# Experts of a pair moved from the last stage of the next pair to the first stage two pairs on, with another split of the first stage's blocks

## The chip, the cores and the metric

One NeuronCore of one Trainium2 chip runs the whole program. The metric is device time in microseconds (us) of one execution; of several runs the median is given. The engines are TensorE (PE, with its weight loads as PEld), VectorE (DVE), ScalarE (ACT), GpSimd (POOL) and the queue engine SyncE (SP), which issues most transfers.

## The reference

A causal convolution along the sequence by FFT, and then a mixture step that changes 128 rows of each sequence.

```python
B, S, D = (8, 6336, 128)          # F = 1024, capacity = 128
Yf = np.fft.rfft(x, n=2 * S, axis=1) * np.fft.rfft(h, n=2 * S, axis=0)[None]
x = np.fft.irfft(Yf, n=2 * S, axis=1)[:, :S, :]
scores = np.einsum('bsd,d->bs', x, w_gate)
out = x.copy()
for b in range(B):
    top_idx = np.argpartition(-scores[b], capacity)[:capacity]
    xe = x[b, top_idx]
    ye = np.maximum(xe @ w1, 0.0) @ w2
    g = 1.0 / (1.0 + np.exp(-scores[b, top_idx]))
    out[b, top_idx] = x[b, top_idx] + g[:, None] * ye
```

## The kernel before

The sequence index is split as n = 64 * n1 + n2, with 99 values of n1 and 64 of n2. Two sequences are worked on at a time, so there are four pairs (`g` = 0 to 3). All products are f32. Each pair goes through four stages, and the order in which instructions stand on every engine is the order in which the Python code writes them: nothing is rescheduled, and each engine takes its instructions strictly in that order. Generators that `yield` are interleaved by `mix(main, (other, rate), ...)`: after each step of `main`, each other generator advances by `rate` steps on the average.

- `stage_a` (products over n1, L159). Its unit is a block of 8 columns of one sequence. POOL turns a block into the buffer `xt` (L143, three buffers, turned up to two blocks ahead), PE multiplies it by `fa` in two steps of 8 matmuls, and ACT or DVE evicts each step's PSUM bank into `slots` (L61 or L63). `acts` is the pattern of who evicts: 1 is ACT, 0 is DVE. A block is named by its half (which sequence of the pair) and by u (which half of the columns). There are 32 blocks in a pair, so 64 steps.
- `stage_b` (products over n2, L57 with the table `w`), 25 steps for each u. Each step needs a table and a piece of the filter's spectrum from HBM, through SP; ACT and DVE multiply by the spectrum (L209, L210, L214), and DVE or POOL adds (L221).
- `stage_c` (products with `wc`, L57), 32 steps for each u, evicted by L61.
- `stage_d` (products over k1 with tables `at`, L247), 32 steps. Each is evicted by ACT (L251), written to `out`, multiplied by `w_gate` on POOL (L255) and summed on DVE (L257). These sums are the scores `ss` of the mixture step.

The mixture step of pair g is the generator `side`, and it runs beside the stages of pair g+1. `pick` finds the 128 largest scores by two searches of eight steps. A step is a chain of DVE compare and reduce (L286, L289), a small PE product with `ones` (L57, into a bank `m` of its own), and three DVE instructions (L293 to L300). `pick` has 28 yields in all. `gather` then fetches the chosen rows with an indirect DMA (L393), and `feed` runs the expert for one sequence: a transpose (L404), 8 products with `w1` (L419), ReLU on ACT (L422), 8 products with `w2` (L427), and a scatter back with an indirect DMA from POOL (L430). Before the change `feed` follows `pick` at once, so the experts of pair g stand in stage d of pair g+1. The mixture step of the last pair has nothing to run beside, and it stands alone at the end of the program: the tail.

The order of a pair after the first is therefore: stage a alone (`part`, 21 blocks, with `side`); stage b for u = 0, with the other 11 blocks of stage a (`more`) between its steps; stage b for u = 1 with stage c for u = 0; stage c for u = 1; stage d.

The two sequences of a pair have their input tiles `xb[0]` and `xb[1]`, which are part of the tile `flat`, named `slots` in the profile. The array `zp` that stage d reads lies over `xb[1]`:

```python
xb = [flat[0:N1, i * XS:(i + 1) * XS].rearrange("p (n d) -> p n d", d=D) for i in range(2)]
yp = flat[:, 2 * XS:].rearrange("p (j k t) -> p j k t", k=N1, t=2)
zp = flat[0:N1, 2 * XS + N1 * 2 * D - ZS:].rearrange("p (j m t) -> p j m t", m=128, t=2)
```

With XS = 8192 and ZS = 32768, `xb[1]` takes the columns 8192 to 16383 and `zp` begins at column 8960. The second sequence of the next pair is loaded by `load_x(x[2 * g + 3], 1)`, which stands after stage d in the program. The first sequence is loaded a stage earlier.

## Time and profile before

| what | value |
|---|---|
| median of 3 runs | 1059.35 us (1058.58 to 1063.21) |
| the profiled execution | 1056.93 us, of which the span of its instructions is 1055.2 us |
| PE busy | 934.0 us (89%), PEld 850.0 us (81%) |
| DVE, ACT, POOL busy | 598.7 us (57%), 574.3 us (54%), 568.8 us (54%) |
| granted TensorE clock | 0.963 of full on the average |
| moved by DMA | 203.18 MB, 193 GB/s on the average |

Busy shares are averages over stages that have different limits. The stages of the pairs follow one another in time, so the trace can be cut at their borders, and each stretch can be read by itself: how long it is, how long each engine was busy in it, the granted clock (1.00 is 2.4 GHz, 0.50 is 1.2 GHz), and the share of the DMA engines' time that was used.

### The profile page before, as it was taken

Reading aid. Unit: us, or ns where it says so; the run is one execution under the profiler, and the core shown is the slowest. Engines: PE = TensorE matmul, PEld = TensorE weight load, DVE = VectorE, ACT = ScalarE, POOL = GpSimd, SP = SyncE. Lnnn points to the kernel's source line nnn. Section 1 sums busy time; section 2 is a strip of 40 time slices with the busy share of each in tenths; the row PEclk is TensorE's granted clock in tenths of the full one; section 3 lists DMA queues with packets and bytes.
Section 4 is the critical chain, followed back from the end, with each engine's and each line's share of the span. In section 5 each row is a group of like instructions: output and inputs, shape, how many; then the busy total and the mean of one; then the engine's idle time right before and its main releaser. Section 6 shows DMA issues by size and latency. Waiting matters only on the chain. (4 is left out here: it accounts for less than half of the span.)

```text
span 1055.2 us, 33274 instructions
## 1 busy us (share of the span) xinstructions
PE 934.0 (89%) x13740; PEld 850.0 (81%) x13740; DVE 598.7 (57%) x1183; ACT 574.3 (54%) x1038; POOL 568.8 (54%) x472
## 2 busy tenths in 40 slices
PE   2998889999999899989999999989999899989614
PEld 2998788997789889977789899967798899967504
DVE  0324677703366978533367978434468887343573
ACT  1324667773357877643367877633378786623201
POOL 2525676505767866126676955037686764056401
PEclk9998999999999999999999999999999999999856
DMA  8787999877775986325575976226567883046300
GB/s 275 256 263 196 248 249 243 227 236 237 251 235 161 298 274 206 144 69 174 158 257 166 309 259 201 102 85 201 171 205 245 275 287 103 2 134 191 99 0 11
DMA packets 121676, 203.18 MB, mean 193 GB/s; under 512 B 12903, under 2 KB 62282, under 8 KB 117962
## 3 DMA queue, kind: packets, MB, share of 16 engines
q1 hardware_dynamic: 94262, 174.05, 54.0%
q10 hardware_dynamic: 26752, 25.96, 7.5%
q8 instruction: 109, 1.79, 0.7%
q0 software_dynamic: 512, 1.05, 0.4%
q14 instruction: 41, 0.34, 0.1%
HBM read 168.05 MB, written 39.45 MB: 197 GB/s over the span
## 5 line engine op out<-in xcount | busy, mean ns | idle before, releaser
L61 ACT COPY slots<-p 128x396 f32<-128x396 f32 (+1 forms) x449 | 263.0, 587 | 130.5 <-PE p L159 63.4
L221 POOL TENSOR_TENSOR slots<-slots,tx 128x512 f32<-128x512 f32 x180 | 232.1, 1306 | 139.0 <-DVE tx L214 95.2
L255 POOL TENSOR_TENSOR tm<-hr,wg 99x512 f32<-99x512 f32 x128 | 161.6, 1275 | 205.3 <-ACT hr L251 169.7
L159 PE MATMUL p<-fa,xt 99*64 99x99 f32 x4608 | 226.8, 252 | 28.4 <-POOL xt L143 20.4
L57 PE MATMUL p<-wc,slots 128*64 128x128 f32 (+1 forms) x4096 | 246.3, 273 | 2.6 <-DVE slots L214 1.9
L57 PE MATMUL p<-slots,w 128*64 128x128 f32 x3168 | 223.2, 282 | 26.0 <-DMA w<-tab_wb 15.8
L159 PEld LDWEIGHTS p<-fa,xt 99*64 99x64 f32 x4608 | 214.5, 139 | 33.0 <-POOL xt L143 21.3
L247 PE MATMUL p<-slots,w 99*99 99x256 f32 x1024 | 231.7, 384 | 3.7 <-ACT slots L61 2.8
L57 PEld LDWEIGHTS p<-wc,slots 128*64 128x64 f32 (+1 forms) x4096 | 228.2, 126 | 5.0 <-DVE slots L214 2.7
L57 PEld LDWEIGHTS p<-slots,w 128*64 128x64 f32 x3168 | 190.0, 138 | 35.0 <-issue 16.2
L247 PEld LDWEIGHTS p<-slots,w 99*99 99x99 f32 x1024 | 168.1, 166 | 60.3 <-ACT slots L61 3.8
L143 POOL COPY xt<-slots 99x512 f32<-99x512 f32 x144 | 165.4, 1169 | 74.1 <-PE p L159 39.7
L257 DVE TENSOR_REDUCE sc<-tm 99x4 f32<-99x512 f32 x128 | 87.6, 686 | 202.7 <-POOL tm L255 202.7
L214 DVE TENSOR_TENSOR slots<-p,hr 128x512 f32<-128x512 f32 (+1 forms) x200 | 136.4, 682 | 80.3 <-ACT p L210 71.1
L251 ACT COPY hr<-p 99x512 f32<-99x512 f32 x128 | 75.0, 586 | 155.3 <-PE p L247 145.6
L209 ACT ACTIVATE p<-p 64x512 f32<-64x512 f32 (+1 forms) x200 | 113.1, 566 | 79.1 <-PE p L57 72.4
L214 DVE TENSOR_TENSOR tx<-p,hr 128x512 f32<-128x512 f32 (+1 forms) x200 | 135.0, 675 | 0.0
L210 ACT COPY p<-p 64x512 f32<-64x512 f32 (+1 forms) x200 | 110.8, 554 | 6.3
L63 DVE COPY slots<-p 128x396 f32<-128x396 f32 (+1 forms) x95 | 58.4, 615 | 43.1 <-PE p L159 42.9
L57 PE MATMUL m<-num,ones 99*64 99x6 bf16 (+1 forms) x112 | 15.6, 182 | 32.5 <-DVE num L289 32.2
L293 DVE TENSOR_SCALAR ge<-m 99x6 f32<-99x6 f32 x64 | 10.4, 163 | 50.2 <-PE m L57 50.2
L57 PEld LDWEIGHTS <-ones 99*64 99x64 bf16 (+1 forms) x112 | 10.1, 111 | 35.2 <-DVE num L289 35.2
(85 smaller groups left out, 390.3 us busy)
## 6 DMA issues: line engine op xcount, KB each, us to landing
w<-tab_wb SPq DMA_DIRECT2D x192, 256.0 KB
hr<-hd SPq DMA_DIRECT2D x144, 256.0 KB
slots<-in_x SPq DMA_DIRECT2D x32, 792.0 KB
out<-hr ACTq DMA_DIRECT2D x128, 198.0 KB
w<-tab_at SPq DMA_DIRECT2D x128, 153.1 KB
hr<-hd SPq DMA_DIRECT2D x96, 128.0 KB
slots<-tab_wb SPq DMA_DIRECT2D x24, 256.0 KB
hd<-hd SPq DMA_DIRECT2D x48, 128.0 KB
```

Source lines behind the costliest of these rows:

```text
L57: nc.tensor.matmul(out[a:b], table[:, a:b], moving, start=start, stop=stop)
L61: nc.scalar.copy(out=dst, in_=src)
L143: nc.gpsimd.tensor_copy(out=xt.rearrange("p d n -> p n d"), in_=xb[half][:, :, d0:d0 + 8])
L159: nc.tensor.matmul(pt[c * 64:(c + 1) * 64, j * N1:(j + 1) * N1], xt[:, q * 4 + j], fa[:, c * N1:(c + 1) * N1], start=True, stop=True)
L209: nc.scalar.mul(out=pw[0:64], in_=pv[64:128], mul=-1.0)
L210: nc.scalar.copy(out=pw[64:128], in_=pv[0:64])
L214: v.tensor_tensor(out=dst, in0=src.rearrange("p k (b j t) -> p k b j t", b=2, t=2), in1=ht[:, t, 0:kn].rearrange("p k (j t) -> p k j t", t ...
L221: (v if adds[ci % len(adds)] else nc.gpsimd).tensor_tensor(out=yv, in0=yv, in1=tx.rearrange("p k (j t) -> p k j t", t=2), op=ALU.add)
L247: nc.tensor.matmul(pt[0:N1, i * 2 * D:(i + 1) * 2 * D], at[:, i % 2, c], zp[:, :, c * N2 + m], start=(c == 0), stop=(c == 1))
L251: nc.scalar.copy(out=yt.rearrange("p b n (u d) -> p (n u) b d", u=2), in_=pt[0:N1].rearrange("p (n b d) -> p n b d", b=nb, d=HD))
L255: nc.gpsimd.tensor_tensor(out=tm, in0=hr[0:N1, o:o + 512].rearrange("p (c d) -> p c d", d=D), in1=wg[0:N1].unsqueeze(1).broadcast_to([N1, ...
L257: v.tensor_reduce(out=ss[:, :, m0:m0 + nd], in_=tm.rearrange("p (b n) d -> p b n d", b=nb), axis=AX.X, op=ALU.add)
```

## The change

The experts leave `side`. `moe` now ends with `gather`, and puts the generator `feed` of its pair on a list, `fed`. In stage a of pair g (from g = 2 on) the experts of pair g-2 are taken from that list and mixed in at 0.35 of a step per step. The experts of pair 2 are mixed into the tail's `pick` at half a step per step, and those of pair 3 end the program. `feed` takes its working tiles from the pool `t` (three buffers) that stages b and d use for `tx` and `tm`, evicts four `w1` products with one ReLU where there were two, and issues its products through the helper `product`.

The share of stage a that runs alone falls from 21 to 17 blocks, so 34 steps, and one eviction in four there goes to DVE. The blocks beside stage b rise from 11 to 15, at 30/24 of a step per step where it was 20/25. In pair 0 the rate beside stage b goes from 30/25 to 32/24. `side` has other rates in every stage.

```diff
-    def feed(b0, nb, picked, new, psm=psm):
+    def feed(b0, nb, picked, new):
         for iu, xe in picked:
-            yield
-            pe = psm()
+            t0 = tp.tile([128, 4, CAP], F32, tag="t", name="fx", bufs=3)
+            pe = bank()
             nc.tensor.transpose(pe[:, 0:CAP], xe, ident)
-            xet = new([D, CAP], F32, "xet")
+            xet, gs = t0[:, 0], t0[:, 1]
...
+            yield
             hm = []
             for f0 in range(0, NF, 4):
-                yield
-                ph = psm().rearrange("p (f t) -> p f t", f=4)
-                for f in range(4):
-                    nc.tensor.matmul(ph[:, f], w1s[:, (f0 + f) * 128:(f0 + f + 1) * 128], xet, start=True, stop=True)
-                for f, tag in ((0, "hf" if f0 else "half"), (2, "m" if f0 else "cmp")):
-                    t = new([128, 2, CAP], F32, tag)
-                    nc.scalar.activation(out=t, in_=ph[:, f:f + 2], func=AF.Relu)
-                    hm += [t[:, 0], t[:, 1]]
-            yield
-            py = psm()
+                ph = bank().rearrange("p (f t) -> p f t", f=4)
+                for f in range(4):
+                    product(ph[:, f], w1s[:, (f0 + f) * 128:(f0 + f + 1) * 128], xet)
+                t = tp.tile([128, 4, CAP], F32, tag="t", name="fh", bufs=3)
+                nc.scalar.activation(out=t, in_=ph, func=AF.Relu)
+                hm += [t[:, f] for f in range(4)]
+                yield
+            py = bank()
...
-    def moe(b0, nb, ss, new, late=3):
+    def moe(b0, nb, ss, new, then):
         p = yield from pick(b0, nb, ss, new)
-        got = gather(b0, nb, p, new)
-        for _ in range(late):
-            yield
-        fs = [feed(b0, nb, got[j:j + 1], new, bank) for j in range(nb)]
-        for f in fs:
-            yield from f
+        then.append(feed(b0, nb, gather(b0, nb, p, new), new))
...
-            part = blocks(0, 0) + blocks(0, 1, 0, 5) + blocks(1, 0)
-            more = blocks(0, 1, 5) + blocks(1, 1)
-            mix(stage_a(part, (1,), more[0:2]), (side, 0.28))
+            part = blocks(0, 0) + blocks(0, 1, 0, 1) + blocks(1, 0)
+            more = blocks(0, 1, 1) + blocks(1, 1)
+            mix(stage_a(part, (1, 1, 1, 0), more[0:2]), (iter(()) if g < 2 else fed.pop(0), 0.35), (side, 0.3))
...
-        mix(stage_b(g, 0, (0, 0, 0, 0, 1)), (a, (2 * len(more) - 2) / 25))
+        mix(stage_b(g, 0, (0, 0, 0, 0, 1)), (a, 2 * len(more) / 24))
...
-        mix(b, (c, 1.33), (side, 0.15))
+        mix(b, (c, 1.33), (side, 0.2))
...
-        mix(stage_c(1, (1,)), (side, 0.36), (twice, 1.0))
+        mix(stage_c(1, (1,)), (side, 0.42), (twice, 1.0))
...
-        mix(itertools.islice(d, 24), (side, 0.45), (twice, 0.8))
+        mix(itertools.islice(d, 24), (side, 0.25), (twice, 0.8))
...
-        side = moe(2 * g, 2, ss, shared)
+        side = moe(2 * g, 2, ss, shared, fed)
         next(side)
     way["columns"] = 128
-    rest(side)
+    mix(side, (fed.pop(0), 0.5))
+    rest(fed.pop(0))
```

How the instructions stand on PE is shown first where stage d of pair 1 ends and stage a of pair 2 begins; L159 is stage a, L247 stage d. Before the change, from the middle of that stage d on:

```order
L247 MATMUL p<-slots,w 99x256 x44
L404 MATMUL p<-tri,xe 128x128
L247 MATMUL p<-slots,w 99x256 x8
L419 MATMUL p<-xet,w1s 128x128 x4
L247 MATMUL p<-slots,w 99x256 x12
L419 MATMUL p<-xet,w1s 128x128 x4
L247 MATMUL p<-slots,w 99x256 x8
L427 MATMUL p<-w2s,half 128x128 x2
...
L427 MATMUL p<-w2s,m 128x128 x2
L159 MATMUL p<-fa,xt 64x99 x120
```

After the change at the same place (L405 is the transpose, and L57 with `fx,w1s` and `w2s,fh` are the experts' products):

```order
L247 MATMUL p<-slots,w 99x256 x128
L159 MATMUL p<-fa,xt 64x99 x24
L405 MATMUL p<-tri,xe 128x128
L159 MATMUL p<-fa,xt 64x99 x24
L57 MATMUL p<-fx,w1s 64x128 x8
L159 MATMUL p<-fa,xt 64x99 x24
L57 MATMUL p<-fx,w1s 64x128 x8
L159 MATMUL p<-fa,xt 64x99 x24
L57 MATMUL p<-w2s,fh 64x128 x16
L159 MATMUL p<-fa,xt 64x99 x16
```

Stage d is 128 products with nothing between them, and its last product is directly followed by stage a. The experts stand between the first 23 of stage a's 34 steps.

On POOL, in stage a of pair 2, `COPY xt` is a block turned, and the indirect `DMA` of L428 is the scatter of one expert. The 21 turns stood in one row before, behind the second scatter of the stage d before it:

```order
L255 TENSOR_TENSOR tm<-hr,wg 99x512 x5
L430 DMA out<-xe,iu 12672x128
L143 COPY xt<-slots 99x64x8 x21
L221 TENSOR_TENSOR slots<-slots,tx 128x4x64x2 x2
L143 COPY xt<-slots 99x64x8
```

After the change:

```order
L255 TENSOR_TENSOR tm<-hr,wg 99x512 x8
L143 COPY xt<-slots 99x64x8 x6
L428 DMA out<-xe,iu 12672x128
L143 COPY xt<-slots 99x64x8 x6
L428 DMA out<-xe,iu 12672x128
L143 COPY xt<-slots 99x64x8 x5
L221 TENSOR_TENSOR slots<-slots,tx 128x4x64x2
L143 COPY xt<-slots 99x64x8
```

The two scatters now stand between the turns, and the turns before stage b fall from 21 to 17. Two more blocks are turned ahead inside stage d in both kernels. The first block of `xb[1]` is number 9 of stage a's own blocks (counted from 0) where it was number 13, so it is the eighth turn of this stretch where it was the twelfth.

On PE at the start of the tail, a search step is the product `m<-num,ones`. Before the change the search steps of the tail stood alone, one after another. After it the experts of pair 2 stand between them:

```order
L405 MATMUL p<-tri,xe 128x128
L57 LDWEIGHTS ones_84
L57 MATMUL m<-num,ones_84 99x6
L57 MATMUL p<-fx,w1s 128x128 x4
L57 LDWEIGHTS ones_84
L57 MATMUL m<-num,ones_84 99x6
L57 LDWEIGHTS ones_84
L57 MATMUL m<-num,ones_84 99x6
L57 MATMUL p<-fx,w1s 128x128 x4
```

The eight pieces of the two experts stand at every second step of `pick`, from its third step on.

## Rows read from the trace of the kernel before

**Rows 1.** Busy time by stretch; starts and ends in us from the span's start.

```profile
core 0: us, PE busy (x) PEld busy (x) DVE busy (x) ACT busy (x) POOL busy (x), PEclk, DMA share, GB/s
96.80:156.40 59.60, 52.60 (x908) 49.92 (x908) 39.38 (x63) 39.51 (x74) 39.88 (x34) 0.92 0.98 246
205.75:238.90 33.15, 32.48 (x596) 32.23 (x592) 3.82 (x8) 23.82 (x38) 3.13 (x3) 1.00 0.76 248
238.90:295.80 56.90, 56.02 (x256) 41.40 (x256) 20.60 (x30) 18.19 (x31) 40.81 (x33) 1.00 0.74 237
295.80:330.80 35.00, 31.80 (x690) 31.13 (x689) 22.42 (x55) 23.12 (x43) 25.63 (x23) 0.95 0.59 189
461.40:531.10 69.70, 65.76 (x328) 50.41 (x328) 28.30 (x55) 22.03 (x45) 45.26 (x37) 0.98 0.55 162
531.10:562.90 31.80, 30.21 (x691) 29.43 (x690) 22.02 (x55) 22.47 (x42) 24.84 (x22) 1.00 0.57 193
562.90:608.50 45.60, 40.11 (x748) 37.89 (x749) 41.05 (x62) 36.23 (x67) 36.07 (x29) 0.99 0.86 285
658.20:693.20 35.00, 33.34 (x584) 31.66 (x584) 14.39 (x45) 22.21 (x35) 2.32 (x2) 1.00 0.22 89
```

**Rows 2.** PE in time, stage d of pair 1; start, length, idle before and releaser.

```profile
473.05 0.18 PE L369 MATMUL m<-lane,cmp 99*128 99x1 bf16 x1 [2.66 <-DVE cmp L363]
...
498.11 1.05 PE L419 MATMUL p<-xet,w1s 128*128 128x128 f32 x8
499.00 5.37 PE L247 MATMUL p<-slots,w 99*99 99x256 f32 x24
...
525.25 1.90 PE L247 MATMUL p<-slots,w 99*99 99x256 f32 x8
...
531.08 10.70 PE L159 MATMUL p<-fa,xt 99*64 99x99 f32 x240
```

**Rows 3.** SP's queue in time: the load of `xb[1]`, pairs 1 and 2.

```profile
296.06 1.72 SPq L80 DMA_DIRECT2D slots<-in_x  x4
...
527.30 1.71 SPq L80 DMA_DIRECT2D slots<-in_x  x4
```

**Rows 4.** POOL in time: the first turn of `xb[1]`, pairs 1 and 2.

```profile
316.64 2.04 POOL L143 COPY xt<-slots 99x512 f32<-99x512 f32 x2 [4.16 <-DMA w<-tab_wb]
...
547.83 1.12 POOL L143 COPY xt<-slots 99x512 f32<-99x512 f32 x1 [0.25 <-PE m L57]
```

**Rows 5.** PE in time, stage a of pair 1.

```profile
314.31 3.92 PE L159 MATMUL p<-fa,xt 99*64 99x99 f32 x48 [1.71 <-issue]
```

**Rows 6.** PE in time, stage b (u = 0) of pair 2 and its end.

```profile
565.43 1.10 PE L57 MATMUL p<-slots,w 128*64 128x128 f32 x16
566.35 0.87 PE L159 MATMUL p<-fa,xt 99*64 99x99 f32 x16
567.03 1.10 PE L57 MATMUL p<-slots,w 128*64 128x128 f32 x16
...
608.52 5.17 PE L57 MATMUL p<-slots,w 128*64 128x128 f32 x64 [1.79 <-issue]
```

**Rows 7.** DVE in time: last score sums of pairs 0 and 3, a gate.

```profile
297.96 0.69 DVE L257 TENSOR_REDUCE sc<-tm 99x4 f32<-99x512 f32 x1 [1.06 <-POOL tm L255]
...
992.06 0.69 DVE L257 TENSOR_REDUCE sc<-tm 99x4 f32<-99x512 f32 x1 [0.57 <-POOL tm L255]
...
1039.67 0.29 DVE L408 TENSOR_TENSOR hit<-xe,wg 128x128 f32<-128x128 f32 x1
...
1040.80 0.16 DVE L413 RECIPROCAL gg<-gg 128x1 f32<-128x1 f32 x1
```

**Rows 8.** PE in time, the tail: a search step, and the first expert.

```profile
1000.16 0.25 PE L57 MATMUL m<-num,ones 99*99 99x6 bf16 x1 [1.83 <-DVE num L289]
...
1040.52 3.78 PE L419 MATMUL p<-xet,w1s 128*128 128x128 f32 x16 [0.35 <-ACT xet L406]
```

**Rows 9.** DVE in time: one instruction in stage a of pair 2 and in the tail.

```profile
532.37 3.61 DVE L270 TENSOR_SCALAR half<-ki 99x128 int32<-99x128 int32 x1
...
993.87 0.23 DVE L270 TENSOR_SCALAR half<-ki 99x128 int32<-99x128 int32 x1
```

More of the change, by code (lines that the diff above doesn't have):

```diff
@@ L397, in gather @@
         return r
-    def feed(b0, nb, picked, new, psm=psm):
+    def feed(b0, nb, picked, new):
         ov = out[0:b0 + nb].rearrange("b s d -> (b s) d")
         for iu, xe in picked:
-            yield
-            pe = psm()
+            t0 = tp.tile([128, 4, CAP], F32, tag="t", name="fx", bufs=3)
+            pe = bank()
             nc.tensor.transpose(pe[:, 0:CAP], xe, ident)
-            xet = new([D, CAP], F32, "xet")
+            xet, gs = t0[:, 0], t0[:, 1]
             nc.scalar.copy(out=xet, in_=pe[:, 0:CAP])
-            gs = new([CAP, D], F32, "hit")
             v.tensor_tensor(out=gs, in0=xe, in1=wg, op=ALU.mult)
@@ L413, in feed @@
             v.reciprocal(out=gg, in_=gg)
+            yield
             hm = []
             for f0 in range(0, NF, 4):
-                yield
-                ph = psm().rearrange("p (f t) -> p f t", f=4)
-                for f in range(4):
-                    nc.tensor.matmul(ph[:, f], w1s[:, (f0 + f) * 128:(f0 + f + 1) * 128], xet, start=True, stop=True)
-                for f, tag in ((0, "hf" if f0 else "half"), (2, "m" if f0 else "cmp")):
-                    t = new([128, 2, CAP], F32, tag)
-                    nc.scalar.activation(out=t, in_=ph[:, f:f + 2], func=AF.Relu)
-                    hm += [t[:, 0], t[:, 1]]
-            yield
-            py = psm()
+                ph = bank().rearrange("p (f t) -> p f t", f=4)
[4 more added lines that the diff above has]
+                hm += [t[:, f] for f in range(4)]
+                yield
+            py = bank()
             for f in range(NF):
-                nc.tensor.matmul(py[:, 0:D], hm[f], w2s[:, f], start=(f == 0), stop=(f == NF - 1))
-            yield
+                product(py[:, 0:D], hm[f], w2s[:, f], f == 0, f == NF - 1)
             v.scalar_tensor_tensor(out=xe, in0=py[:, 0:D], scalar=gg[:, 0:1], in1=xe, op0=ALU.mult, op1=ALU.add)
@@ L488, in conv_moe @@
     twice = stage_twice()
+    fed = []
     for g in range(G):
@@ L519, in conv_moe @@
                 turn(bl)
-        mix(d, (side, 0.45))
+        mix(d, (side, 0.25))
         rest(side)
```

## The prediction

> **What bounds the kernel now.** I read the stretches first, because the mean shares hide them [rows 1]. PE is the limit wherever it has work: 56.0 of 56.9 us in stage d of pair 0, and 30.2 of 31.8 us in stage a of pair 2. The exceptions are three. Beside stage b (u = 0) PE is busy for only 40.1 of 45.6 us, and DVE (41.1), ACT (36.2), POOL (36.1) and the transfers (0.86) are all close behind. Stage a of pair 1 takes 35.0 us for the steps that take 31.8 us in pair 2. And the tail is a chain, not a load.
>
> Second, PE in time within stage d. Stage d takes 69.7 us in pair 1 and 56.9 us in pair 0, which has no mixture step beside it [rows 1]. The 12.8 us between them are the experts' products, small products of `pick`, and waits, of which the longest is 2.66 us, for a DVE instruction queued behind the score sums [rows 2].
>
> Third, the load of `xb[1]`, which is invisible in the busy times. In pair 1 SP issues it at 296.06 us [rows 3], 0.2 us after stage d ends, since `zp` lies over `xb[1]`. The first turn that needs it starts at 316.64 us, after POOL sat idle for 4.16 us [rows 4]. The profile names a table as the releaser, but the turn reads only `xb[1]`, which came through the same queue. So 20.6 us pass from issue to turn. PE waits 1.71 us there and runs the next 48 records in 3.92 us [rows 5], which is the half clock: 16 records take 0.68 us beside stage b (566.35 to 567.03) [rows 6]. In pair 2 the load is issued at 527.30 us, 3.8 us before stage a begins at 531.08 us, because the experts' last products still run after the last read of `zp` [rows 2, 3]. The same turn then starts at 547.83 us with no wait for data [rows 4]. This load just fits now, with 13 blocks ahead of it.
>
> **The change part by part.** All terms are against the profiled execution's own 1056.93 us; the median of the runs is 2.4 us above it, and I add that at the end.
>
> *Stage d of pairs 1 to 3.* The experts leave. Eight records take 0.89 us (498.11 to 499.00) [rows 2], so 0.111 us each; an expert has 33 records (1 transpose, 16 with `w1`, 16 with `w2`), 3.7 us, and a pair 7.3 us. By the new rates `pick` has used its 28 yields when stage d begins (1 + 10 + 4 + 13), so its products and their waits leave too. I take pair 0's stage d as the new length: -12.8 us in pairs 1 and 2. The low bound is the products alone, -7.3. In pair 3 something comes back. The last sum of scores ends 2.85 us after stage d's last product when nothing stands behind it (297.96 + 0.69 against 295.80) [rows 1, 7]; in pair 3 before, the experts covered it, and the sum ended at 992.75 us, as they did [rows 7]. So -9.9 there. Together **-35.5**.
>
> *Stage c.* It takes two more steps of `pick`. Eleven steps cost 35.0 - 33.15 = 1.85 us [rows 1], 0.17 each. At 0.42 some steps follow after only two products, some 1.9 us, where a search step alone takes 1.83 + 0.25 = 2.08 us [rows 8]; eight such gaps are at most 1.2 us of waits. I take 0.8 a pair: **+2.4** (0.3 to 1.5 each). One more step beside stage b (u = 1): **+0.5**.
>
> *Stage a alone.* Four blocks leave, which is 8 x 0.68 = 5.4 us of PE. But the first block of `xb[1]` is now block 9, and stage d ends without experts behind it, so in every pair the load starts as in pair 1: its turn begins 0.2 + 20.6 us into the stage, and its product 1.1 us later, at 21.9. PE arrives there after 18 steps, 12.2 us, in pair 1. In pairs 2 and 3 six of the eight expert pieces (42 records, 4.7 us) stand ahead too: 16.9 us. So it waits in all three. Behind it come 16 steps (10.9), five search products (0.9), the last eviction (0.6) and half a microsecond of low clock: 34.8 us, against 35.0 in pair 1. The gain is nothing there, because the load decided before as well. In pairs 2 and 3 there are two more expert pieces (24 records, 2.7) and about 1 us in which POOL holds the second scatter ahead of a turn: 38.5 against 31.8, so +6.7 each. Together **+13.4** (each pair from 3 us less to 3 us more). Whatever else is late in the first 18 steps costs nothing, since the load covers 5 to 10 us: DVE's quarter of the evictions behind the 3.6 us instruction [rows 9], the gates, the first scatter. Without this cover it would be about 2 us a pair.
>
> On the gates the trace and a rule can be weighed. One and the same DVE instruction takes 3.61 us beside POOL's turns and 0.23 us in the tail [rows 9]. The Trainium skill (SBUF — State Buffer, Who interferes with whom) says that DVE and GpSimd share a port pair as an exclusive lock, and that a DVE instruction with two inputs in SBUF contends with a GpSimd instruction that reads SBUF. The gate's product `xe * wg` is one, and it moves in among the turns; an estimate by that rule is a turn's 1.12 us for each of four gates, 4.5 us, and the forecast would be 1053.5 if none were covered. By the order, all four stand ahead of block 9, so I add nothing.
>
> *Beside stage b (u = 0).* A step of b takes 0.92 us and a step of a 0.68 us of PE [rows 6]. Now 25 and 22 of them are 38.0 us in a stretch of 45.6, with 7.6 us of waits; 25 and 30 are 43.4. The waits shrink: a step of b with its share of a has 1.74 us where it had 1.52, so its tables have longer to arrive, and the 1.79 us wait at the end [rows 6] goes, as the last step of a now stands ahead of the last of b. Against that, DVE gets two more evictions and POOL four more turns. Bounds: 1 us of waits (44.4) and all of the old ones (51.0). I take 3.9, about half, 47.3: +1.7 a pair, **+5.1**. In pair 0 the transfers are full (0.98) [rows 1]; the four steps of a left over at its end, 2.7 us, now fit between: **-2** (0 to -3.5).
>
> *The tail.* The experts of pair 2 join the search chain. PE idles 1.83 us in each search step [rows 8]. A gate holds DVE for 1.29 us (1039.67 to 1040.96) [rows 7], twice, and the last addition 0.35, twice: 3.3 us. Four `w1` pieces of 8 records fit. A `w2` piece of 16 records is 1.78 us at the full clock, and 3.78 us at the half clock that the tail shows [rows 8], 1.95 over the gap, twice. So 3.3 to 7.4; nothing excludes more, up to all records at half clock with the gates, 17. I take **+5.5**. The experts of pair 3 end the program as before, at 0.
>
> The sum: -35.5 + 2.4 + 0.5 + 13.4 + 5.1 - 2 + 5.5 = -10.6, so 1046.3 us, and 1048.7 beside the median: **1049 us**, 1% faster.
>
> **The rivals.**
>
> *The load does not decide.* The transfers use only 0.59 of their time in stage a [rows 1], so the load could land sooner with stage d shorter. Then PE sets the pace: pair 1's stage a falls to 31.8 - 5.4 = 26.4 us (8.4 less than I have), pairs 2 and 3 to 33.7 (4.8 less): 18 us less, 1031. The load would have to land within some 12 us in pair 1; both pairs shown took about 20 from issue to turn.
>
> *The gain is eaten beside stage b.* If all old waits stay there, each pair takes 51.0 us: +11, 1060, no change. DVE's 41.1 of 45.6 us speaks for it; the transfers' slack of 0.14 and the vanishing last wait speak against.
>
> *Slower: stage b (u = 0) falls to pair 0's pace.* There the same mix, 25 steps of b beside a full load of a, takes 59.6 us [rows 1]. At that pace in pairs 1 to 3 it is 3 x 12.3 = 37 us more, 1086. It decides from about 52 us a pair on, where the sum crosses +0.5%. Against it: the transfers were at 0.98 there and are at 0.86 here.
>
> That the change does not do what it says is excluded by the order: no expert and no search product stands in stage d any more.
>
> **How the numbers follow.** The forecast has 0.60, the early load 0.12, the eaten gain 0.20, the slower rival 0.08. The forecast's own bounds (stage a, stage b and the tail) give 1041 to 1057. The range takes in the eaten gain and leaves out the slower rival and most of the early load: 1038 to 1062. Half a per cent, 5.3 us, is about what this measurement can tell from no change, so the borders are 1054 and 1064.6. Faster: 0.12 and 0.54 of the forecast, 0.66. Same: 0.06 of the forecast and 0.16 of the eaten gain, 0.22. Slower: 0.08 and 0.04, 0.12.
>
> **What would show it.** Stage d of pairs 1 to 3 at 56 to 58 us each with PE busy throughout. In stage a POOL idles before its eighth turn until some 21 us into the stage, in all three pairs, and the stage takes 35, 38 and 38 us. Stage b (u = 0) takes 47 us without the wait at its end. The tail's search steps of 2.08 us are stretched where experts stand. I am wrong if the eighth turn starts without a wait, if stage b (u = 0) exceeds 52 us, or if the tail grows by more than 10 us.

## The result, and the profile after

The changed kernel takes 1044.82 us (median of 4 runs, 1042.93 to 1046.74) against 1061.28 us of the kernel before, measured beside it. The ratio is 0.9856, with a 95% interval of 0.9809 to 0.9903; executions in a slower state, into which some runs fall, are left out of it, so it is not the quotient of the two medians. Measured again on another chip (changed_again below), it is 0.9879 (0.984 to 0.9917). The profiled execution took 1044.07 us, with a span of 1042.3 us: 12.9 us less than the span before.

PE's work is the same as before. The first lines of the page of the changed kernel:

```profile
span 1042.3 us, 33485 instructions
...
PE 935.9 (90%) x13868; PEld 849.3 (81%) x13868; DVE 601.4 (58%) x1213; ACT 553.7 (53%) x992; POOL 566.0 (54%) x472
```

PE was busy for 934.0 us before and is for 935.9 us now. So between these two executions the whole gain is idle time of PE: 121.2 us before, 106.4 us now. That is the question to put to every move below: whether it takes away a wait, or only carries work from one place to another.

Busy time by stretch of the changed kernel (columns as in [rows 1]): stage d of pair 0, stage a of pair 1, stage d of pair 1, stage a and stage b (u = 0) of pair 2, stage c (u = 1) of pair 2, stage a of pair 3, and the end from stage d's last product on:

```profile
core 0: us, PE busy (x) PEld busy (x) DVE busy (x) ACT busy (x) POOL busy (x), PEclk, DMA share, GB/s
235.80:296.30 60.50, 58.03 (x258) 42.35 (x258) 20.58 (x30) 18.20 (x32) 40.83 (x33) 0.97 0.71 228
296.30:330.80 34.50, 27.78 (x559) 26.89 (x558) 21.41 (x53) 14.46 (x27) 20.17 (x19) 0.90 0.55 190
463.90:520.90 57.00, 55.87 (x258) 41.56 (x258) 21.65 (x35) 18.19 (x32) 42.75 (x35) 1.00 0.62 188
520.90:557.50 36.60, 32.52 (x689) 31.04 (x688) 25.79 (x63) 16.14 (x35) 22.26 (x21) 1.00 0.54 184
557.50:602.60 45.10, 44.32 (x876) 43.19 (x876) 37.40 (x62) 37.85 (x71) 38.71 (x32) 1.00 0.83 263
651.30:689.90 38.60, 36.79 (x636) 34.15 (x632) 19.14 (x59) 24.16 (x39) 3.63 (x3) 1.00 0.24 95
...
747.10:782.70 35.60, 32.27 (x690) 31.03 (x690) 25.61 (x63) 16.08 (x35) 22.22 (x21) 1.00 0.56 188
972.20:1042.30 70.10, 31.05 (x166) 27.21 (x164) 41.22 (x143) 7.14 (x17) 7.37 (x8) 0.66 0.04 11
```

Stage d of pair 1 fell from 69.7 us [rows 1] to 57.0, and its granted clock rose from 0.98 to 1.00. Stage a rose from 31.8 us to 36.6 in pair 2 and from 30.8 to 35.6 in pair 3, and stayed near its 35.0 in pair 1 (34.5). Stage b (u = 0) has PE busy for 44.32 of 45.10 us, where it was busy for 40.11 of 45.60.

PE in time in the changed kernel, answering to [rows 2, 5, 6, 8]; start, length, and in brackets the idle time before and its releaser:

```profile
242.85 19.23 PE L247 MATMUL p<-slots,w 99*99 99x256 f32 x80 [1.55 <-DMA w<-tab_at]
...
315.22 4.23 PE L159 MATMUL p<-fa,xt 99*64 99x99 f32 x48 [4.58 <-POOL xt L143]
...
319.31 3.42 PE L159 MATMUL p<-fa,xt 99*64 99x99 f32 x48
...
322.57 2.26 PE L159 MATMUL p<-fa,xt 99*64 99x99 f32 x48
...
540.71 2.27 PE L159 MATMUL p<-fa,xt 99*64 99x99 f32 x48 [0.81 <-POOL xt L143]
551.84 0.19 PE L57 MATMUL m<-num,ones 99*64 99x6 bf16 x2 [2.01 <-DVE num L289]
551.89 2.93 PE L159 MATMUL p<-fa,xt 99*64 99x99 f32 x64
...
605.91 2.42 PE L57 MATMUL p<-slots,w 128*64 128x128 f32 x32 [1.08 <-DMA w<-tab_wb]
...
985.01 0.25 PE L57 MATMUL m<-num,ones 99*99 99x6 bf16 x1
987.09 0.25 PE L57 MATMUL m<-num,ones 99*99 99x6 bf16 x1 [1.83 <-DVE num L289]
987.20 3.72 PE L57 MATMUL p<-w2s,fh 128*128 128x128 f32 x16
990.75 0.17 PE L57 MATMUL m<-num,ones 99*99 99x6 bf16 x1
```

In pair 1 PE waits 4.58 us for the first turned block of `xb[1]`, and then runs two groups of 48 records in 4.23 and 3.42 us, where the third takes 2.26: the granted clock is 0.50 over the first group and 0.63 over the second, and about 3 us are lost by it. In pair 2 the same wait is only 0.81 us and in pair 3 there is none, but in both a new one stands further on, for a search step's count on DVE (2.01 us in pair 2, 11 us behind the first, and 2.02 us in pair 3). In the tail, the search step that starts behind a `w2` piece comes 3.66 us after the one before it (987.09 to 990.75), where 2.08 us is usual (985.01 to 987.09).

SP's queue, POOL and DVE in time in the changed kernel, answering to [rows 3, 4, 7]:

```profile
296.49 1.75 SPq L80 DMA_DIRECT2D slots<-in_x  x4
...
521.09 1.77 SPq L80 DMA_DIRECT2D slots<-in_x  x4
```

```profile
314.12 2.89 POOL L143 COPY xt<-slots 99x512 f32<-99x512 f32 x3 [6.45 <-DMA hr<-hd]
...
539.59 4.19 POOL L143 COPY xt<-slots 99x512 f32<-99x512 f32 x4 [2.60 <-DMA w<-tab_wb]
544.73 1.33 POOL L143 COPY xt<-slots 99x512 f32<-99x512 f32 x1 [0.95 <-PE p L159]
547.70 0.98 POOL L428 DMA_INDIRECT out<-xe,iu  x1 [1.64 <-DVE xe L427]
548.69 2.03 POOL L143 COPY xt<-slots 99x512 f32<-99x512 f32 x2
```

```profile
544.34 0.17 DVE L300 TENSOR_TENSOR thr<-ge,cst 99x6 f32<-99x6 f32 x1
...
548.63 1.98 DVE L300 TENSOR_TENSOR thr<-ge,cst 99x6 f32<-99x6 f32 x1
...
974.15 0.69 DVE L257 TENSOR_REDUCE sc<-tm 99x4 f32<-99x512 f32 x1 [1.05 <-POOL tm L255]
...
976.33 0.28 DVE L408 TENSOR_TENSOR fx<-xe,wg 128x128 f32<-128x128 f32 x1
...
977.39 0.16 DVE L413 RECIPROCAL gg<-gg 128x1 f32<-128x1 f32 x1
```

The load of `xb[1]` takes 17.6 us from issue to turn in pair 1 (296.49 to 314.12) and 18.5 us in pair 2 (521.09 to 539.59). The 2.01 us wait of PE begins on DVE: L300 makes six new thresholds, which takes 0.17 us at 544.34 and 1.98 us at 548.63. The second time it runs beside two turns that POOL carries out in one row, because the scatter held them up.

### The profile page after: what moved, and what is told of

Same layout as the page of the kernel before. It is cut to its first block, busy times and chain, and to the rows that moved or that the text cites. A ratio compares the mean times of both kernels' runs of the same rounds, so it can differ in the third digit from the quotient of the medians.

```text
span 1042.3 us, 33485 instructions
## 1 busy us (share of the span) xinstructions
PE 935.9 (90%) x13868; PEld 849.3 (81%) x13868; DVE 601.4 (58%) x1213; ACT 553.7 (53%) x992; POOL 566.0 (54%) x472
## 5 line engine op out<-in xcount | busy, mean ns | idle before, releaser
L61 ACT COPY slots<-p 99x512 f32<-99x512 f32 (+1 forms) x419 | 244.6, 590 | 148.9 <-PE p L159 84.3
L159 PE MATMUL p<-fa,xt 99*64 99x99 f32 x4608 | 232.1, 253 | 28.7 <-POOL xt L143 27.1
L57 PE MATMUL p<-wc,slots 128*64 128x128 f32 (+1 forms) x4096 | 247.1, 273 | 4.1 <-DVE slots L214 3.0
L159 PEld LDWEIGHTS p<-fa,xt 99*64 99x64 f32 x4608 | 216.3, 139 | 34.7 <-POOL xt L143 31.1
L57 PE MATMUL p<-slots,w 128*64 128x128 f32 x3168 | 221.3, 279 | 19.1 <-DMA w<-tab_wb 12.7
L57 PEld LDWEIGHTS p<-wc,slots 128*64 128x64 f32 (+1 forms) x4096 | 226.7, 126 | 8.3 <-DVE slots L214 4.5
L247 PE MATMUL p<-slots,w 99*99 99x256 f32 x1024 | 225.8, 380 | 8.0 <-DMA w<-tab_at 5.2
L247 PEld LDWEIGHTS p<-slots,w 99*99 99x99 f32 x1024 | 166.9, 164 | 66.1 <-issue 4.7
L57 PEld LDWEIGHTS p<-slots,w 128*64 128x64 f32 x3168 | 185.9, 136 | 26.2 <-issue 10.6
L63 DVE COPY slots<-p 128x396 f32<-128x396 f32 (+1 forms) x125 | 75.1, 603 | 53.6 <-PE p L159 51.2
L57 PE MATMUL m<-num,ones 99*64 99x6 bf16 (+2 forms) x112 | 13.4, 183 | 30.0 <-DVE num L289 29.3
L428 POOL DMA_INDIRECT out<-xe,iu x8 | 8.0, 1004 | 54.4 <-DVE ge L296 36.3
L289 DVE TENSOR_REDUCE num<-cmp 99x6 bf16<-99x384 bf16 x64 | 35.4, 553 | 2.2
```

Of the source, the lines that this page charges most:

```text
L57: nc.tensor.matmul(out[a:b], table[:, a:b], moving, start=start, stop=stop)
L61: nc.scalar.copy(out=dst, in_=src)
L63: v.tensor_copy(out=dst, in_=src)
L159: nc.tensor.matmul(pt[c * 64:(c + 1) * 64, j * N1:(j + 1) * N1], xt[:, q * 4 + j], fa[:, c * N1:(c + 1) * N1], start=True, stop=True)
L247: nc.tensor.matmul(pt[0:N1, i * 2 * D:(i + 1) * 2 * D], at[:, i % 2, c], zp[:, :, c * N2 + m], start=(c == 0), stop=(c == 1))
```

## The experiments

The theory after the first reading: stage d gets shorter because both `pick` and the experts leave it; the load of `xb[1]` sets the pace of stage a, and covers most of the experts there. The rivals: one of the two departures pays alone; or PE's work or another wait sets the pace of stage a. Each kernel ran beside the kernel before on the same chip.

**split_only.** The kernel before with the new split of stage a.

```diff
-            part = blocks(0, 0) + blocks(0, 1, 0, 5) + blocks(1, 0)
-            more = blocks(0, 1, 5) + blocks(1, 1)
-            mix(stage_a(part, (1,), more[0:2]), (side, 0.28))
+            part = blocks(0, 0) + blocks(0, 1, 0, 1) + blocks(1, 0)
+            more = blocks(0, 1, 1) + blocks(1, 1)
+            mix(stage_a(part, (1, 1, 1, 0), more[0:2]), (side, 0.33))
...
-        mix(stage_b(g, 0, (0, 0, 0, 0, 1)), (a, (2 * len(more) - 2) / 25))
+        mix(stage_b(g, 0, (0, 0, 0, 0, 1)), (a, 2 * len(more) / 24))
```

> The kernel before with the new split alone: 17 blocks in stage a, 15 beside stage b, the new evictions and rates there; experts and pick stay where they were. Theory (experts and pick leaving stage d are the gain, the split is worth next to nothing): stage a of pair 1 stays at 34 to 35 us, because the load of xb[1] ends it; in pairs 2 and 3 it falls by about 1 us, since the load starts 3.8 us earlier there; stage b (u = 0) falls by less than 1 us and what follows it gains as much. Total within 3 us of before, ratio 0.997 to 1.003. Rival (more work beside stage b is the gain): stage a falls by 5 us in each pair and stage b stays, ratio about 0.986 or lower.

Ratio 1.0036 (0.9997 to 1.0075), just above what was expected: nothing gained. The profiled execution took 1073.69 us, about 10 us more than the median of this kernel, so only one thing is read from it: PE still waits for the load, 3.90 us in pair 1 and 4.99 us in pair 2.

**experts_only.** The changed kernel with the old split (21 and 11 blocks, and the evictions and rates that belong to it), so the experts and `pick` are moved, the blocks are not.

```diff
-            part = blocks(0, 0) + blocks(0, 1, 0, 1) + blocks(1, 0)
-            more = blocks(0, 1, 1) + blocks(1, 1)
+            part = blocks(0, 0) + blocks(0, 1, 0, 5) + blocks(1, 0)
+            more = blocks(0, 1, 5) + blocks(1, 1)
-            mix(stage_a(part, (1, 1, 1, 0), more[0:2]), (iter(()) if g < 2 else fed.pop(0), 0.35), (side, 0.3))
+            mix(stage_a(part, (1,), more[0:2]), (iter(()) if g < 2 else fed.pop(0), 0.28), (side, 0.25))
...
-        mix(stage_b(g, 0, (0, 0, 0, 0, 1)), (a, 2 * len(more) / 24))
+        mix(stage_b(g, 0, (0, 0, 0, 0, 1)), (a, (2 * len(more) - 2) / 25))
```

> The changed kernel with the old split (21 and 11 blocks, all evictions of stage a alone on ACT, old rates beside stage b). Theory: stage d 57 us in pairs 1 to 3 as in the changed kernel; stage a 35 us in pair 1, about 38.5 us in pairs 2 and 3 (42 steps, experts 7.3 us, no wait for the load); stage b (u = 0) back to 45.6 us with its 1.8 us wait at the end. Total 0 to 3 us above the changed kernel, ratio 0.985 to 0.989. Rival (the split is the gain): ratio 0.997 or more.

Ratio 0.9864 (0.9816 to 0.9912), the changed kernel's within the interval. Stage a takes 32.6, 41.1 and 41.1 us; in pair 2 PE is busy for 38.0 of them at full clock, and no wait reaches 1 us. So the split adds nothing in this company either.

**old_side_rates.** The changed kernel, but `pick` advances at the old rates and so ends in stage d again.

```diff
-            mix(stage_a(part, (1, 1, 1, 0), more[0:2]), (iter(()) if g < 2 else fed.pop(0), 0.35), (side, 0.3))
+            mix(stage_a(part, (1, 1, 1, 0), more[0:2]), (iter(()) if g < 2 else fed.pop(0), 0.35), (side, 0.33))
...
-        mix(b, (c, 1.33), (side, 0.2))
+        mix(b, (c, 1.33), (side, 0.15))
...
-        mix(stage_c(1, (1,)), (side, 0.42), (twice, 1.0))
+        mix(stage_c(1, (1,)), (side, 0.36), (twice, 1.0))
...
-        mix(itertools.islice(d, 24), (side, 0.25), (twice, 0.8))
+        mix(itertools.islice(d, 24), (side, 0.45), (twice, 0.8))
...
-        mix(d, (side, 0.25))
+        mix(d, (side, 0.45))
```

> The changed kernel with the old rates of side, so that pick's last steps stand in stage d again and the experts do not. Theory: of the 12.6 us by which stage d fell, 7.3 are the experts' products and the rest are pick's products, PE's waits for DVE behind the score sums, and half clock after them: stage d of pairs 1 to 3 at 60 to 62 us, 1 us less in stage c, total 6 to 12 us above the changed kernel, ratio 0.991 to 0.997. Rival (the experts alone made stage d long): stage d 57 to 58 us, ratio 0.984 to 0.987.

Ratio 1.0002 (0.9965 to 1.0039): the whole gain is gone, more than the theory's 0.991 to 0.997, though all experts are out of stage d. Two stretches of this kernel, stage d of pair 1 and stage a of pair 2, and a row of PE in that stage d:

```profile
463.80:525.40 61.60, 58.28 (x264) 42.70 (x266) 25.20 (x44) 18.17 (x32) 42.86 (x35) 0.97 0.59 174
527.70:564.70 37.00, 32.05 (x644) 30.63 (x643) 28.69 (x67) 14.88 (x32) 19.82 (x19) 0.95 0.49 172
```

```profile
475.43 0.18 PE L369 MATMUL m<-lane,cmp 99*128 99x1 bf16 x1 [2.66 <-DVE cmp L363]
```

Stage d takes 61.6 us: the end of `pick` costs 4.6 us there, with the same 2.66 us wait as before [rows 2] and part of the stage at the half clock (granted 0.85 from 475.4 to 487.0 us, 0.97 over the stage). The 8.1 us that stage d lost with the experts came back: stage a of pair 2, from 525.32 to 564.67, takes 39.35 us against 31.8. Stage a of the three pairs is also 1.0, 2.8 and 1.3 us longer here than in the first profile of the changed kernel, which takes the loss beyond the theory's; why it is, stays open.

**pick_only.** The converse: the kernel before, but `pick` advances faster and ends before stage d. The experts stay in stage d, and the split is the old one.

```diff
-            mix(stage_a(part, (1,), more[0:2]), (side, 0.28))
+            mix(stage_a(part, (1,), more[0:2]), (side, 0.25))
...
-        mix(b, (c, 1.33), (side, 0.15))
+        mix(b, (c, 1.33), (side, 0.2))
...
-        mix(stage_c(1, (1,)), (side, 0.36), (twice, 1.0))
+        mix(stage_c(1, (1,)), (side, 0.42), (twice, 1.0))
...
-        mix(itertools.islice(d, 24), (side, 0.45), (twice, 0.8))
+        mix(itertools.islice(d, 24), (side, 0.42), (twice, 0.8))
...
-        mix(d, (side, 0.45))
+        mix(d, (side, 0.42))
```

> The kernel before with faster rates for side: pick ends before stage d, and the experts stay in stage d; the split of stage a and everything else is as before. Theory (after e3): what pays is that pick leaves stage d, whichever place the experts have. Then stage d of pairs 1 to 3 takes 64 to 65 us where it took 69.7 (the experts' products stay, 7.3 us), stage c takes 1 us more in each pair, stage b (u = 1) 1 us more, the tail is as before: a gain of 3 to 9 us, ratio 0.990 to 0.997. Rival: pick and experts must both leave for a gain, since the experts' chain then stalls by itself in stage d: stage d at 68 us or more, ratio 1.000 or above.

Ratio 0.9846 (0.9803 to 0.9889), while the changed kernel on the same chip had 0.9879 (0.984 to 0.9917). The rates of `side` in four stages give the whole gain. The stretches of stage d of pair 1 with the experts' last products, and of stage a of pair 2:

```profile
467.00:530.20 63.20, 63.18 (x324) 49.17 (x324) 25.23 (x45) 22.01 (x44) 45.03 (x37) 1.00 0.60 175
530.20:561.70 31.50, 29.84 (x689) 29.27 (x688) 22.29 (x47) 22.45 (x42) 24.45 (x23) 1.00 0.59 203
```

PE is busy for 63.18 of 63.20 us: the experts in stage d stall nothing. What stalled was the end of `pick`. The gain, 6.5 us of stage d, is more than I had expected (5), and the ratio lies below the theory's 0.990 to 0.997.

**changed_again.** The changed kernel as it is, beside pick_only.

> The changed kernel itself, unchanged, beside the three others on their chip. Both theories: ratio 0.981 to 0.990, with stage d of pairs 1 to 3 at 56 to 57 us, and stage a at 34 to 35 us in pair 1 and 35 to 39 us in pairs 2 and 3. What it tells is how far stage a and the tail move from one profile of the same kernel to the next.

Ratio 0.9879 (0.984 to 0.9917), span 1041.2 us. Stage a of pair 2 takes 38.6 us here (519.67 to 558.31) and 36.6 in the first profile, so 2 us of one stage is what one execution differs from the next, and it can be more: in tables_later, whose edit came to nothing (below), the same stage takes 41.3 us.

**no_load_wait.** In pairs 1 to 3 the blocks of the second sequence are turned from `xb[0]`, so that no turn waits for the load of `xb[1]`; the second sequence's output is then that of the first.

```diff
-        nc.gpsimd.tensor_copy(out=xt.rearrange("p d n -> p n d"), in_=xb[half][:, :, d0:d0 + 8])
+        nc.gpsimd.tensor_copy(out=xt.rearrange("p d n -> p n d"), in_=xb[half if way.get("own", True) else 0][:, :, d0:d0 + 8])
...
+            way["own"] = False
```

> The changed kernel, but in pairs 1 to 3 the blocks of the second sequence are turned from the first sequence's tile, so that they wait for no load (the second sequence's output is then the first's); the load itself is still made. Theory, by the waits of the changed kernel's trace (4.58 us in pair 1, 0.81 in pairs 2 and 3, and a stretch of half clock in pair 1): stage a 29 to 31 us in pair 1, 35 to 36 in pairs 2 and 3; total 6 to 8 us below the changed kernel, ratio 0.978 to 0.981. Rival (my recorded sum, about 5 us of wait in each of pairs 2 and 3): 12 to 16 us below, ratio 0.971 to 0.974.

Ratio 0.9849 (0.9796 to 0.9903). Stage a of pair 1 falls to 27.0 us (296.71 to 323.68): the load is its price there. In pair 2 the stage does not fall, it takes 40.8 us (512.08 to 552.83). The stretch, the waits of PE, and the instruction behind the first of them on DVE:

```profile
512.00:552.90 40.90, 35.68 (x691) 34.46 (x692) 27.46 (x63) 16.43 (x35) 22.00 (x21) 0.92 0.50 165
```

```profile
531.13 0.19 PE L57 MATMUL m<-num,ones 99*64 99x6 bf16 x2 [1.90 <-DVE num L289]
...
545.52 0.22 PE L57 MATMUL m<-num,ones 99*64 99x6 bf16 x2 [2.02 <-DVE num L289]
```

```profile
527.18 2.72 DVE L300 TENSOR_TENSOR thr<-ge,cst 99x6 f32<-99x6 f32 x1
```

With the load out of the way, the waits for the search's counts decide, and the half clock behind them: the granted clock is 0.92, and PE is busy for about 3 us more than in the changed kernel's stage a (35.7 against 32.5). Neither of the two theories had it.

**no_experts.** The changed kernel with the experts left out; the chosen rows stay unchanged in the output.

```diff
-            mix(stage_a(part, (1, 1, 1, 0), more[0:2]), (iter(()) if g < 2 else fed.pop(0), 0.35), (side, 0.3))
+            mix(stage_a(part, (1, 1, 1, 0), more[0:2]), (side, 0.3))
...
-    mix(side, (fed.pop(0), 0.5))
-    rest(fed.pop(0))
+    rest(side)
```

> The changed kernel with the experts left out everywhere, in stage a, in the tail and at the end; the rows are still chosen and fetched, but not changed, so the output lacks the mixture step. Theory (the load covers a part of the experts in stage a): stage a of pairs 2 and 3 takes about 34.5 us as in pair 1 (2 and 1 us less), the tail is about 16 us shorter: 19 us less than the changed kernel, ratio about 0.968. Rival (PE sets the pace in stage a, and each expert product there costs its whole time): stage a of pairs 2 and 3 takes about 29 us, 7.3 less each, in all 31 us less, ratio about 0.957.

Ratio 0.962 (0.9572 to 0.9668), span 1023.2 us: 19.1 us less than the profile of the changed kernel, the theory's size; the ratio lies between the two. Stage a of pair 2 by stretch, PE and POOL in it:

```profile
519.70:556.40 36.70, 26.56 (x561) 25.68 (x560) 21.46 (x53) 14.47 (x27) 20.48 (x19) 0.91 0.58 179
```

```profile
542.12 4.07 PE L159 MATMUL p<-fa,xt 99*64 99x99 f32 x48 [8.02 <-POOL xt L143]
```

```profile
541.01 2.93 POOL L143 COPY xt<-slots 99x512 f32<-99x512 f32 x3 [9.88 <-DMA slots<-in_x]
```

The stage is as long without the experts (36.7 us) as with them (36.6, and 38.7 in changed_again). PE waits 8.02 us for the load in place of them, and then runs 48 records in 4.07 us. So the experts cost next to nothing in the new stage a of pair 2, but only because the new split leaves a hole of 8 us there.

**tables_later.** The changed kernel, but the first tables and filter pieces of the next stage b are asked for at the 17th step of stage a.

```diff
-            mix(stage_a(part, (1, 1, 1, 0), more[0:2]), (iter(()) if g < 2 else fed.pop(0), 0.35), (side, 0.3))
+            mix(late(stage_a(part, (1, 1, 1, 0), more[0:2]), 16, ("b", g, 0, 0)), (iter(()) if g < 2 else fed.pop(0), 0.35), (side, 0.3))
...
-            ahead(("b", g + 1, 0, 0))
```

> The changed kernel, but the first tables and filter pieces of the next stage b are asked for at the 17th step of stage a and not at the end of stage d, so that they do not share the transfers with the load of xb[1]. Theory (the load decides stage a of pair 1, and the lock of DVE beside POOL's turns decides pairs 2 and 3): stage a of pair 1 takes about 31 us where it took 34.5, pairs 2 and 3 stay at 36 to 39; in all 1 to 5 us less than the changed kernel, ratio about 0.982 against the kernel before. Rival (tables and load do not hinder one another, or the tables then come late for stage b): no gain against the changed kernel or 1 to 3 us more, ratio 0.986 to 0.989.

Ratio 0.9898 (0.9841 to 0.9954), but the edit did not do what it says: SP has nothing else in its queue there and runs ahead of the other engines, so the tables still went out at 298.26 us (298.29 in the changed kernel), right behind the load at 296.57. PE's wait in pair 1 stayed at 4.75 us. What the tables take from the load stays open.

**sum_in_psum.** The changed kernel, but the sum from which L300 makes the thresholds lies in PSUM, and a second sum for the next step is made off the chain.

```diff
+                if late:
+                    v.tensor_reduce(out=ge[:, :, 3], in_=late, axis=AX.X, op=ALU.add)
...
-                v.tensor_reduce(out=up[:, :, 3], in_=ge, axis=AX.X, op=ALU.add)
+                if it < 7:
+                    sums = pt[0:N1, 128:128 + nb].rearrange("p (b j) -> p b j", j=1)
+                    v.tensor_reduce(out=sums[:, :, 0], in_=ge, axis=AX.X, op=ALU.add)
+                    late = ge
...
-                    v.tensor_tensor(out=thr, in0=ge[:, :, 3:4].broadcast_to([N1, nb, 3]),
+                    v.tensor_tensor(out=thr, in0=sums.broadcast_to([N1, nb, 3]),
```

> The changed kernel, but in a search step the sum that the next thresholds are built from is written to PSUM, so that the addition that makes the thresholds has one input in PSUM and one in SBUF; a second sum for the next step goes to SBUF behind the count, off the chain. Theory (the addition, 0.17 us elsewhere, is held for 1.98 us by POOL's turns in stage a of pairs 2 and 3, and PE's 2.0 us wait for the search product comes from that): the addition stays under 0.5 us there, the 2.0 us waits go, stage a of pairs 2 and 3 falls by 1 to 2.5 us each, and the tail grows by at most 3 us (14 further sums of 0.16 us): between no change and 4 us less than the changed kernel. Rival (DVE is held whatever the inputs are, as the one-input instruction of L270 was): the 1.98 us stay on this or the neighbouring instruction, stage a as in the changed kernel, total 0 to 3 us more.

Ratio 0.9863 (0.9812 to 0.9914), no gain. DVE in time in stage a of pair 2, POOL and PE beside it:

```profile
548.05 0.17 DVE L308 TENSOR_TENSOR thr<-m,cst 99x6 f32<-99x6 f32 x1
548.25 2.17 DVE L287 TENSOR_TENSOR cmp<-hf,thr 99x384 bf16<-99x384 f32 x1
```

```profile
548.10 2.04 POOL L143 COPY xt<-slots 99x512 f32<-99x512 f32 x2
```

```profile
551.05 0.19 PE L57 MATMUL m<-num,ones 99*64 99x6 bf16 x2 [1.81 <-DVE num L290]
551.10 4.22 PE L159 MATMUL p<-fa,xt 99*64 99x99 f32 x64
```

The addition is free now: all 56 of them take 0.17 us, where 8 of 56 took 1.16 us or more in the changed kernel. The hold went to the next instruction, the comparison (0.56 us elsewhere, 2.17 here), whose two inputs are in SBUF. The rival is right that the wait stays, on the neighbouring instruction, but not that the inputs do not matter. The Trainium skill (SBUF — State Buffer, Who interferes with whom) says that a DVE instruction with two SBUF inputs contends with a GpSimd instruction that reads SBUF, and that one with at most one, outside the modes in which it uses two ports, does not. These two rows agree.

**w2_in_halves.** The changed kernel, but in the tail an expert's products with `w2` are issued in two pieces at two steps of `pick`.

```diff
                 product(py[:, 0:D], hm[f], w2s[:, f], f == 0, f == NF - 1)
+                if cut and f == 3:
+                    yield
...
-        then.append(feed(b0, nb, gather(b0, nb, p, new), new))
+        then.append(feed(b0, nb, gather(b0, nb, p, new), new, b0 == 4))
```

> The changed kernel, but in the tail an expert's products with w2 are issued in two pieces, four products at one step of pick and four at the next. Theory (the 3.7 us w2 piece at the half clock does not fit into a search step and holds the search chain): the tail's search steps with w2 pieces fall to the length of the others, the tail is 2.5 to 4 us shorter, in all about 3 us less than the changed kernel. Rival (the gates and the additions on DVE make the tail's price): tail as in the changed kernel, no gain.

Ratio 0.9806 (0.9768 to 0.9845), the lowest of all kernels that leave nothing out, though its interval overlaps with those of the changed kernel. The end from stage d's last product on, and PE in it:

```profile
972.70:1038.40 65.70, 30.69 (x166) 26.31 (x164) 41.31 (x143) 7.15 (x17) 7.46 (x8) 0.63 0.04 12
```

```profile
987.69 0.24 PE L57 MATMUL m<-num,ones 99*99 99x6 bf16 x1 [1.83 <-DVE num L289]
987.79 2.06 PE L57 MATMUL p<-w2s,fh 128*128 128x128 f32 x8
989.77 0.25 PE L57 MATMUL m<-num,ones 99*99 99x6 bf16 x1
991.85 0.24 PE L57 MATMUL m<-num,ones 99*99 99x6 bf16 x1 [1.83 <-DVE num L289]
```

Each search step takes 2.08 us again (987.69 to 989.77 to 991.85), and the end is 4.4 us shorter than the changed kernel's 70.1 (the theory had 2.5 to 4).

**pick_only_tail.** pick_only, with the experts of pair 2 in the tail, in the same halves (`apart` is the changed kernel's `feed`); those of pairs 0 and 1 stay in stage d.

```diff
+        if b0 == 4:
+            then.append(apart(b0, nb, got, new, True))
+            return
...
-    rest(side)
+    mix(side, (fed.pop(0), 0.5))
```

> The kernel of the run pick_only (pick ends before stage d, the experts of pairs 0 and 1 stay in stage d, the old split), but the experts of pair 2 run in the tail beside the search, with w2 in two pieces. Theory (the middle of the program is bound by PE's work there, the tail has idle PE): stage d of pair 3 falls by 4.5 to 7.5 us (57 to 54 us with the last sums of scores), the tail grows by 1.5 to 3.5 us, so 2 to 5 us less than pick_only, ratio 0.980 to 0.984. Rival (a tail step costs as much as PE gains): ratio as pick_only, 0.985 or more.

Ratio 0.9821 (0.9776 to 0.9865). Stage d of pair 3, and the program from its end on:

```profile
916.80:973.80 57.00, 55.95 (x257) 41.73 (x258) 21.67 (x35) 18.19 (x31) 41.00 (x33) 1.00 0.63 188
973.80:1041.10 67.30, 32.29 (x166) 28.07 (x164) 41.23 (x143) 7.39 (x21) 7.45 (x8) 0.59 0.04 11
```

The first takes 57.0 us in place of 61.3 in pick_only, and the second 67.3 us in place of 65.7: as expected, about 3 us by the two profiles. The ratios of the two kernels (0.9821 and 0.9846) cannot tell them apart.

**sum_and_halves.** Both edits, sum_in_psum and w2_in_halves, in the changed kernel.

> The changed kernel with both edits, the sum in PSUM and w2 in two pieces in the tail. Theory: the two add up, 3 to 7 us less than the changed kernel, ratio 0.979 to 0.984. Rival (neither is a bound): 0.986 or more.

Ratio 0.984 (0.9803 to 0.9876), span 1037.5 us. The end takes 66.3 us, as in w2_in_halves (65.7), and stage a 34.2, 37.4 and 35.4 us, as in the changed kernel: what is gained is the halves' gain, and that the two edits add up is not shown.

## Why the prediction was right, and where it was not

The direction, the time (1049 forecast) and the range held. By its own terms, in us (stage borders at the first product of the next stage, so that stage b (u = 0) reaches to stage c's first; pair 3's stage d and the tail at the last sum of scores):

| term | forecast | measured |
|---|---|---|
| stage d, pairs 1 to 3 | -35.5 | -35.4 |
| stage c | +2.4 | +2.8 |
| beside stage b (u = 1) | +0.5 | +3.4 |
| beside stage b (u = 0) | +5.1 | +1.8 |
| stage a | +13.4 | +9.1 |
| pair 0 | -2 | +0.4 |
| the tail | +5.5 | +5.0 |
| sum | -10.6 | -12.9 |

That the sum came within 2.3 us is in part luck: four of the terms missed by 2.4 to 4.3 us, two to either side.

**Stage d** was sized rightly: 57.0 us, pair 0's length, with the last sum of pair 3 exposed (974.15 + 0.69). But the sum never asked which of the two departures pays, and that is the weak place of the argument. The runs that differ by one part tell it:

| kernel | `pick` in stage d | experts in stage d | split | ratio |
|---|---|---|---|---|
| split_only | yes | yes | new | 1.0036 |
| old_side_rates | yes | no | new | 1.0002 |
| pick_only | no | yes | old | 0.9846 |
| experts_only | no | no | old | 0.9864 |
| changed, twice | no | no | new | 0.9856, 0.9879 |

In these rows the ratio goes with the first column alone. `pick`'s end cost 4.6 us in stage d (61.6 against 57.0), of which 2.66 us is one wait, and the half clock behind it makes most of the rest. Its steps cost less where they stand now: stage c takes two more of them and grew by 0.9 us a pair, and the stretch beside stage b (u = 1) takes one more and grew by 1.1. The experts' products are 7.3 us of PE wherever they stand. From stage d's first product in pair 1 to stage c's first in pair 2, pick_only takes 144.1 us (467.02 to 611.07), the changed kernel 144.2 (463.96 to 608.13), and no_experts 144.0 (464.08 to 608.03); a pair later it is 142.6, 144.1 and 141.4. So moving the experts mainly fills a hole which the new split had made. The experts of pair 2 are the same exchange: stage d of pair 3 is 4.9 us shorter in the changed kernel than in pick_only (56.4 against 61.3), and the end 4.4 us longer (70.1 against 65.7), until w2_in_halves takes that back.

**Stage a**, +13.4 forecast, +9.1 measured: the mis-sized step. The load decides pair 1, as said (34.5 us measured, 34.8 forecast; PE's wait 4.58). In pairs 2 and 3 the forecast had PE waiting 5 us for it. The load was quicker (in pair 2 the product came 19.8 us into the stage, 540.71 less 520.9, and not 21.9), and PE came later (at 19.0, not 16.9), so only 0.81 us was left in pair 2 and nothing in pair 3. The forecast had taken about 20 us as the load's time from both pairs before, but in pair 2 the turn had not waited for data [rows 4], so its 20.5 us were only an upper bound. In its place stands the wait of 2.01 and 2.02 us for the search's count. The cover that I had relied on ("whatever else is late in the first 18 steps costs nothing") ends at the load; this wait stands behind it. I had weighed the lock of DVE and POOL for the gates alone. They stood ahead of block 9 as the forecast had it, and their products took 0.28 us each (at 527.97 and 537.96 us), not held at all; the price came from an addition of 6 elements a partition behind the scatter. How much of the 2 us wait would go with that hold is not shown: in sum_in_psum the hold only went to the next instruction.

**Beside stage b**, the two terms together are +5.2 against +5.6 forecast, but differently shared: the waits of stage b (u = 0) went almost wholly (PE busy for 44.32 of 45.10 us), and some came back at the start of stage b (u = 1), such as the 1.08 us for a table at 605.91. The 3.4 us beside stage b (u = 1), where the forecast had 0.5, belong to `pick`'s further step: pick_only, with the old split, has 3.5 us more there than the kernel before, and old_side_rates has none. The rival in which the gain is eaten there, and the one that falls to pair 0's pace, are both refuted.

**Pair 0**: its stage d began 3.1 us sooner (235.87 against 238.9 [rows 1]) and waited for its tables instead, 1.55 us at 242.85 and 0.60 and 0.25 later. In changed_again it began at 239.78 us, later than before, and took 57.4 us. So the 2 us are not shown in either execution; where they were won, they were given back, and the forecast had not asked what is late next.

**The tail**: the forecast's mechanism (a `w2` piece of 3.78 us at the half clock against a gap of 1.83) is what the rows show (3.72), and w2_in_halves takes 4.4 us of it away. The gate takes 1.2 us (976.33 to 977.55), as from [rows 7].

**The early load** did not come in the changed kernel. no_load_wait shows what it would have been: 27.0 us in pair 1 (that rival had 26.4), but 40.8 us in pair 2 (it had 33.7), since the search's waits and the half clock take over.

Where the experts stand in stage a without a load wait, its 39 to 41 us add up. In no_load_wait, pair 2, they are 35.7 us of PE's work, part of it at the half clock, and waits of 1.90, 2.02, 0.70 and 0.59 us. In experts_only they are 38.0 us of work, with eight more steps, and four waits of together 3.2 us. Open: why the clock fell behind these waits in some executions and not in others; and how much of the load's 17 to 21 us is due to the tables beside it.

## What to carry to other kernels

When several things leave a full stage at once, ask of each whether it stalls the engine there or only uses it. Work that only uses PE is as dear in the next place, unless PE waits there; a chain of small steps through another engine is dear where that engine's queue is held and cheap where it is not. Here the rates in four stages did what the whole change did. And a piece that is dropped into the gaps of a serial chain has to be shorter than a gap, at the clock which holds there.

## What the runs showed of the hardware

A DVE instruction on six elements a partition was held for 1.98 us, and in no_load_wait for 2.72, beside POOL's turns of about 1 us each, where it takes 0.17 elsewhere: at 548.63 it was held until about 0.1 us before the end of both turns of a row (548.69 for 2.03). So a tiny instruction on a serial chain can pay for a whole row of copies. Both rows had formed behind a scatter that held POOL. It is not always the whole row: at 540.55 in the changed kernel a comparison that takes 0.56 us elsewhere took 1.31 us beside a row of four turns (539.59 for 4.19). That the addition with one input in PSUM takes 0.17 us each time, and that the next instruction is held (2.17 us), was shown by sum_in_psum.

PE's clock after a wait of 2 us was not always the same: 64 records took 2.93 us behind a wait of 2.01 (granted clock 1.00, 2.4 GHz), and 4.22 us behind one of 1.81 in sum_in_psum (granted 0.84 and then 0.50, 1.2 GHz), 13 us after another wait, of 1.87 us.

SP ran ahead of the other engines: in tables_later the program asks for the tables 17 steps later, and they were issued at 298.26 us, where it was 298.29 in the changed kernel.
